# Attention output of two head groups on column tiles of TensorE

## The chip, the cores and the metric

The kernel runs on one core of a Trainium2 chip. The metric is the device time of one execution in microseconds (us), lower is better. A core has TensorE (PE in the profile; its weight loads are listed as PEld), VectorE (DVE), ScalarE (ACT), GpSimd (POOL) and the DMA queues, among them SyncE's (SP), which run beside each other and wait for one another through semaphores.

TensorE keeps a block of weights (`lhsT`) in its array and streams another operand (`rhs`) through it; each matmul has its own weight load. The result goes to PSUM: the columns of `lhsT` become PSUM partitions. The array can be used whole (128 rows by 128 columns) or cut into tiles that are addressed by `tile_position=(row, column)`. A tile of 32x64 takes 32 rows of contraction and 64 weight columns, and its output lies on 64 PSUM partitions.

## The reference

A transformer block on `x` of 2048 x 1024, everything stored in bfloat16: 32 heads of 32 values, causal attention with a window of 256, then a dense layer pair with SiLU.

```python
def _A_ref(x, wqkv, wo):
    B, S, D = x.shape
    H = 32; Dh = D // H; W = 256
    qkv = (x @ wqkv) ...            # split in q, k, v by head
    scores = einsum("bhqd,bhkd->bhqk", q, k) * Dh ** -0.5
    mask = (idx[:, None] - idx[None, :] >= 0) & (idx[:, None] - idx[None, :] < W)
    p = softmax(where(mask, scores, -1e9))
    o = einsum("bhqk,bhkd->bhqd", p, v)
    return o.reshape(B, S, D) @ wo
def _B_ref(x, w1, w2):
    return silu(x @ w1) @ w2
h = x + _A_ref(layernorm(x), wqkv, wo)
out = h + _B_ref(layernorm(h), w1, w2)
```

## The kernel before

The 2048 rows are cut into four blocks of 512 (`b` = 0 to 3), the 32 heads into eight head groups of four (`g` = 0 to 7). The program runs in stages; in each, dense matmuls of one block carry the attention of the block before it:

- first the q, k and v of block 0 (lines 497 to 581);
- the attention of block 0 among the q, k, v of block 1 (lines 587 to 601);
- the attention of block 1 among the q, k, v of block 2, and that of block 2 among those of block 3 (the loop at line 604). Block 2's attention is what the change calls the third stage: it is the third of the four blocks, and its code has `b == 2`;
- the attention of block 3 among the output projections of blocks 0 to 2 (line 639 on);
- then the dense layers, `h1_group` (line 666) and `mm2` (line 704), for all four blocks.

The order of the work is written out by hand and nothing reorders it. The class `Stream` (line 415) sets how attention is mixed into the dense matmuls. A stage has 24 dense groups of eight matmuls, 192 in all; before each dense matmul `between` is called, and at even distances, 20 times in a stage of blocks 1 to 3, it issues a piece of attention output and then a burst of scores. So PE's stream in such a stage is a repeated triple: one piece (`attn_piece`), one burst of scores, and nine or ten dense matmuls.

Scores are computed by `scores_xy` (line 288) on tiles of 32 rows by 64 columns: four heads of the group on four row tiles, two halves of 64 keys on two column tiles, 24 matmuls a burst with 320, 128 and 64 streamed columns. The parts that two neighbouring groups need at the window's edge come from `scores_c` (line 321), every fifth burst, 16 matmuls on tiles of 32x128. ACT takes the exponential of the scores from PSUM (`sc`) into a ring in SBUF (`r_e`), and POOL zeroes what the mask excludes (`select`, line 371).

`attn_out` (line 377) multiplies probabilities by values. `lhsT` is a block of 128 keys by 128 queries, so queries become output partitions; `rhs` is `v` for one head, 32 values and a column of ones that gives the softmax's sum: 33 columns. For one head and 128 queries three such matmuls accumulate in one slot of `o_ps`. A head group has 16 slots (four heads, four query tiles), 48 matmuls. Two neighbouring groups, 32 slots, are cut by `SPLIT` (line 41) into five pieces of 8, 8, 5, 6 and 5 slots; the group with the even number is in the first two, 24 matmuls each. A piece is issued four bursts after the scores it belongs with. After eight slots `attn_norm` (line 392) has DVE divide by the sums, and `attn_transpose` turns the result by DMA.

Weight loads wait for POOL (the mask), the first matmul of a slot bank for DVE (the division before), the first score of a burst for ACT (the exponentials before). These waits stand in PE's own queue.

Of the kernel before, what the change touches and what calls it, by code (L numbers as in the profile page):

```python
# [14 lines left out]
P = 128  # L15
# [22 lines left out]
    [(0, "X", 2), (1, "Y", 1), (2, "X", 3)],  # L38
    [(1, "Y", 2), (2, "C", 1), (3, "Y", 3)],
]  # L40
SPLIT = [(0, 8), (8, 16), (16, 21), (21, 27), (27, 32)]


@with_exitstack
def kernel(
# [10 lines left out]
    nc = tc.nc  # L56
# [12 lines left out]
    VW = DH + 1  # L69
# [22 lines left out]
    o_ps = [ps.tile([P, 8, 64], F32, name=f"o_ps{i}") for i in range(2)]  # L92
    acc_ps = [ps.tile([P, 512], F32, name=f"acc{i}") for i in range(2)]

    def view(region, off, *dims):
        n = 1
        for d in dims:
            n *= d
        ap = region[:, off:off + n]
        if len(dims) == 2:  # L100
            return ap.rearrange("p (a b) -> p a b", b=dims[1])
        if len(dims) == 3:
            return ap.rearrange("p (a b c) -> p a b c", b=dims[1], c=dims[2])
        return ap
# [12 lines left out]
    v = view(r_a, 32768, S // P, H, VW)  # L117
# [113 lines left out]
    def next_acc():  # L231
        acc_n[0] += 1
        return acc_banks[acc_n[0] % len(acc_banks)]
# [45 lines left out]
    def chunk_of(i, bank, piece, pair, hh):  # L279
        if bank == "C":  # L280
            return c_ring[:, (i + 1) % 3, pair * 2 + hh, piece * P:(piece + 1) * P]
        if i < G:
            c0 = hh * 512 + piece * P
        else:
            c0 = 1024 + hh * P if piece == 2 else hh * 512 + (piece - piece // 3) * P
        return xy_ring[(i % 2 * 2 + "XY".index(bank)) * 2 + pair][:, c0:c0 + P]

    def scores_xy(b, g, odd):
        q0 = odd * P
        mid, first, last = odd, odd - 2, odd + 2  # L290

        parts = [
            (mid, 0, q0, q0 + 320, 64), (mid, 1, q0 + 64, q0 + 384, 128),
            (last, 0, q0 + 256, q0 + 384, 384), (first, 1, q0, q0 + 128, 0),
            (first, 0, q0, q0 + 64, 0), (last, 1, q0 + 320, q0 + 384, 448),
        ]
        for step in range(3):
            for hh in range(4):
                for kt, half, qa, qb, col in parts[step * 2:step * 2 + 2]:
                    r0 = hh * DH  # L300
                    t = b * 4 + kt
                    k0 = (t % 4) * P + half * 64
                    nc.tensor.matmul(  # L303
                        sc[hh // 2][half * 64:half * 64 + 64, hh % 2, col:col + qb - qa],
                        lhsT=kT[t // 4][r0:r0 + DH, g, k0:k0 + 64],
                        rhs=qT[b][r0:r0 + DH, g, qa:qb],
                        start=True, stop=True, tile_position=(r0, half * 64),
                    )
        for pair in range(2):
            e = xy_ring[((b * G + g) % 2 * 2 + odd) * 2 + pair]  # L310
            tri = e[:, 0:1024].rearrange("p (h c q) -> p h c q", h=2, q=256)
            bank = sc[pair]
            both = bank[:, :, 0:192]
            both = bass.AP(tensor=both.tensor, offset=both.offset, ap=[*both.ap[:2], [320, 2], both.ap[2]])
            nc.scalar.activation(out=tri[:, :, :, 64:256], in_=both, func=ACT.Exp, scale=scale)  # L315
            nc.scalar.activation(out=e[:, 1024:1280].rearrange("p (h q) -> p h q", q=P), in_=bank[:, :, 192:320], func=ACT.Exp, scale=scale)  # L316
            four = e[:, 0:1024].rearrange("p (c q) -> p c q", q=256)
            select(four[:, :, 0:P], four[:, :, 64:64 + P], False)
            select(four[:, :, P:2 * P], four[:, :, P:2 * P], True)
# [57 lines left out]
    def attn_out(b, g, first, last):  # L377
        i = b * G + g
        for n in range(first, last):
            pair, qt, hh = n // 8, n // 2 % 4, n % 2  # L380
            chunks = (CHUNKS if b else CHUNKS_0)[qt]
            for m, (kt, bank, piece) in enumerate(chunks):
                nc.tensor.matmul(  # L383
                    o_ps[pair][:, qt * 2 + hh, 0:VW],
                    lhsT=chunk_of(i, bank, piece, pair, hh),
                    rhs=v[:, b * 4 + kt, g * 4 + pair * 2 + hh, :],
                    start=(m == 0), stop=(m == len(chunks) - 1),
                )
            if n % 8 == 7:
                attn_norm(i, pair)  # L390

    def attn_norm(i, pair):
        recip = small.tile([P, 8, 1], F32, name="recip", tag="recip")
        nc.vector.reciprocal(out=recip[:], in_=o_ps[pair][:, :, DH:VW])
        nc.vector.tensor_tensor(
            out=obuf[i % 3][:, :, pair * 64:(pair + 1) * 64].rearrange("p t (h d) -> p t h d", d=DH),
            in0=o_ps[pair][:, :, 0:DH].rearrange("p (t h) d -> p t h d", h=2),
            in1=recip[:].rearrange("p (t h) o -> p t h o", h=2).to_broadcast([P, 4, 2, DH]), op=ALU.mult,
        )
# [6 lines left out]
    def attn_piece(b, g, first, last):  # L406

        for k in range(2):
            a, z = max(first - 16 * k, 0), min(last - 16 * k, 16)
            if a < z:  # L410
                attn_out(b, g + k, a, z)
                if z == 16:
                    late.append(lambda k=k: attn_transpose(b, g + k))

    class Stream:
# [3 lines left out]
        def __init__(self, b):  # L419
# [4 lines left out]
            for g in range(0, G, 2):  # L424
                if b:
                    self.bursts += [lambda g=g: scores_c(b, g)]
                    self.bursts += [lambda g=g, k=k, o=o: scores_xy(b, g + k, o) for k in range(2) for o in range(2)]
                    self.pieces += [lambda g=g, s=s: attn_piece(b, g, *s) for s in SPLIT]
                else:
# [86 lines left out]
    pair = [next_acc() for _ in range(2)]  # L516
# [166 lines left out]
    for b in range(NB):  # L683
# [4 lines left out]
        for ft in range(FT):  # L688
# [8 lines left out]
            if b == 0 and 7 <= ft < 15:  # L697
                j, c = divmod(ft - 7, 2)
# [60 lines left out]
```

## Time and profile before

| | |
|---|---|
| time, median of 3 runs | 691.2 us (690.91 to 691.21) |
| profiled execution, first to last instruction (span) | 688.9 us |
| PE busy | 685.2 us, 99% of the span |
| DVE, ACT, POOL busy | 42%, 35%, 23% |
| attention output, all 1440 matmuls of 128x33 (line 383) | 48.1 us busy, 178 ns mean of one |
| stage of block 2's attention | 163.3 to 223.4 us from the span's start |
| its pieces for groups 2 and 4 | start at 190.4, 193.4, 205.4 and 208.4 us |

The page gives no other time for the profiled execution than its span; the median of the timed runs is 2.3 us above that span. A row of the profile names the line of the kernel, the engine, the operation, what it writes and reads by the program's names, the array tile (`128*128` or `32*64`) and the shape of the streamed operand, then how many. The duration of one matmul is from its start to its modelled end; matmuls overlap, so the distance from one start to the next is shorter than the duration: 25 ns for the 128x33 matmuls that are listed with 178 ns. The chain lists what ended last, piece by piece in order of time.

### The profile page before, as it was taken

The numbers are of one execution on the slowest core, as the hardware profiler recorded it, in microseconds if no ns is written. First come the engines' busy times: TensorE is split into PE (matmuls) and PEld (weight loads), VectorE is DVE, ScalarE is ACT, GpSimd is POOL, SyncE is SP. The second block draws the span as 40 slices with busy tenths as digits, with TensorE's granted clock in tenths as the row PEclk, the third lists the DMA queues.
The fourth block names the chain that finished last, engine by engine and source line by source line (L and its number), as shares of the span: only waits on it lengthen the run. The fifth ranks groups of instructions, "written<-read, shape, count | busy, mean of one in ns | idle before, by whom it ended". The sixth has DMA issues, their size and how long they took to land.

```text
span 688.9 us, 14243 instructions
## 1 busy us (share of the span) xinstructions
PE 685.2 (99%) x6011; PEld 342.3 (50%) x6011; DVE 291.2 (42%) x613; ACT 244.2 (35%) x464; POOL 160.8 (23%) x295
## 2 busy tenths in 40 slices
PE   9999999999999999999999999999999999999998
PEld 4445555555555555544444444444444444444445
DVE  5267647744444449444316133342233251333111
ACT  7326666666667666421300033300133100233000
POOL 1006666566666656400000000000000000000000
PEclk9999999999999999999999999999999999999999
DMA  7832231126241889871023310022300123100110
GB/s 259 275 64 69 40 85 57 25 63 186 71 131 21 257 252 272 199 267 40 23 88 112 84 39 0 1 91 70 85 0 1 21 96 90 39 1 1 30 39 24
DMA packets 78641, 61.48 MB, mean 89 GB/s; under 512 B 52465, under 2 KB 62705, under 8 KB 78577
## 3 DMA queue, kind: packets, MB, share of 16 engines
q1 hardware_dynamic: 77888, 59.78, 30.2%
q8 instruction: 47, 0.77, 0.4%
q10 hardware_dynamic: 688, 0.79, 0.3%
q14 instruction: 18, 0.14, 0.1%
HBM read 39.85 MB, written 8.39 MB: 70 GB/s over the span
## 4 chain that ended last, share of the span: by engine, by line
PE 99%; DVE 0%; issue 0%
PE hacc L669 19%; PE hacc L706 18%; PE acc L250 17%; PE acc L706 11%; PE acc L669 9%; PE acc L240 7%; PE acc L271 7%; PE o_ps L383 5%; PE sc L303 3%; PE hacc L271 2%; PE sc L355 1%; PE o_ps L240 1%; PE o_ps L167 1%; PE sc L329 1%; PE acc L525 0%; PE o_ps L525 0%
## 5 line engine op out<-in xcount | busy, mean ns | idle before, releaser
L373 POOL TENSOR_SCALAR_AFFINE_SELECT r_e<-r_e 128x512 bf16<-128x512 bf16 (+1 forms) x288 | 157.8, 563 | 123.9 <-ACT r_e L363 60.8
L706 PEld LDWEIGHTS <-r_a 128*128 128x128 bf16 x952 | 90.9, 98 | 103.0
L669 PEld LDWEIGHTS <-r_w 128*128 128x128 bf16 x896 | 87.3, 98 | 104.8
L706 PE MATMUL hacc<-r_a 128*128 128x512 bf16 (+2 forms) x616 | 122.5, 360 | 0.0
L669 PE MATMUL hacc<-r_e,r_w 128*128 128x512 bf16 x456 | 100.9, 379 | 0.0
L315 ACT ACTIVATE r_e<-sc 128x768 bf16<-128x768 f32 x96 | 78.2, 814 | 47.9 <-PE sc L303 47.9
L678 ACT ACTIVATE r_n<-hacc 128x512 f32<-128x512 f32 x30 | 17.9, 597 | 178.9 <-PE hacc L669 178.9
L250 PEld LDWEIGHTS <-r_w 128*128 128x128 bf16 x512 | 47.1, 98 | 55.0 <-issue 1.0
L706 PE MATMUL acc<-r_a 128*128 128x512 bf16 x336 | 74.0, 379 | 0.0
L252 DVE CAST r_a<-acc 128x512 bf16<-128x512 f32 x56 | 38.7, 692 | 57.7 <-PE acc L250 57.4
L250 PE MATMUL acc<-r_t,r_w 128*128 128x512 bf16 x256 | 59.6, 380 | 0.0
L250 PE MATMUL acc<-r_w 128*128 128x512 bf16 x256 | 57.8, 380 | 0.0
L383 PEld LDWEIGHTS <-r_e 128*128 128x128 bf16 x1440 | 47.4, 96 | 17.9
L669 PE MATMUL acc<-r_e,r_w 128*128 128x512 bf16 x216 | 49.1, 379 | 0.0
L271 PE MATMUL acc<-r_o,r_a 128*128 128x512 bf16 x208 | 48.7, 380 | 0.0
L383 PE MATMUL o_ps<-r_a,r_e 128*128 128x33 bf16 x1440 | 48.1, 178 | 0.0
L721 DVE SCALAR_TENSOR_TENSOR r_t<-hacc,r_t 128x512 bf16<-128x512 f32 (+2 forms) x22 | 14.0, 635 | 56.7 <-PE hacc L706 56.7
L316 ACT ACTIVATE r_e<-sc 128x256 bf16<-128x256 f32 x96 | 37.6, 392 | 0.0
L271 PEld LDWEIGHTS <-r_a 128*128 128x128 bf16 x256 | 23.4, 98 | 26.9
L721 DVE SCALAR_TENSOR_TENSOR r_t<-acc,r_t 128x512 bf16<-128x512 f32 x12 | 8.3, 692 | 64.2 <-PE acc L706 64.2
L679 DVE SCALAR_TENSOR_TENSOR r_a<-r_n,hacc 128x512 bf16<-128x512 f32 x30 | 20.6, 687 | 33.0 <-ACT r_n L678 33.0
L669 PE MATMUL hacc<-r_a,r_w 128*128 128x512 bf16 x144 | 33.0, 379 | 0.0
(100 smaller groups left out, 539.6 us busy)
## 6 DMA issues: line engine op xcount, KB each, us to landing
r_w<-in_B_w_dram SPq DMA_DIRECT2D x8, 896.0 KB, 5.2
r_a<-in_B_w_dram SPq DMA_DIRECT2D x7, 1024.0 KB, 7.5
r_w<-in_A_wqkv_dram SPq DMA_DIRECT2D x4, 1024.0 KB, 7.8
h_dram<-r_t SPq DMA_DIRECT2D x16, 256.0 KB, 3.1
r_t<-h_dram SPq DMA_DIRECT2D x16, 256.0 KB, 2.8
out_dram<-r_t SPq DMA_DIRECT2D x31, 128.0 KB, 1.7
r_o<-in_A_x_dram SPq DMA_DIRECT2D x15, 256.0 KB, 4.6
r_e<-h_dram SPq DMA_DIRECT2D x3, 1024.0 KB, 5.7
```

The costliest lines, as they stand in the source:

```text
L240: nc.tensor.matmul(acc, lhsT=lnT_b[b % 2][:, kt, j * P:(j + 1) * P], rhs=wv[:, kt, c * 512:(c + 1) * 512], start=(kt == 0), stop=(kt == KT ...
L250: nc.tensor.matmul(acc, lhsT=wqk[:, kt, col0:col0 + P], rhs=lnT_b[b % 2][:, kt, :], start=(kt == 0), stop=(kt == KT - 1))
L252: copy(out=(qT, kT)[which][b][:, g, :], in_=acc)
L271: nc.tensor.matmul(acc, lhsT=qT[b][:, g, j * P:(j + 1) * P], rhs=wo[:, g, c * 512:(c + 1) * 512], start=(g == 0), stop=(g == G - 1))
L303: nc.tensor.matmul(sc[hh // 2][half * 64:half * 64 + 64, hh % 2, col:col + qb - qa], lhsT=kT[t // 4][r0:r0 + DH, g, k0:k0 + 64], rhs=qT[b] ...
L315: nc.scalar.activation(out=tri[:, :, :, 64:256], in_=both, func=ACT.Exp, scale=scale)
L316: nc.scalar.activation(out=e[:, 1024:1280].rearrange("p (h q) -> p h q", q=P), in_=bank[:, :, 192:320], func=ACT.Exp, scale=scale)
L373: nc.gpsimd.affine_select(out=dst, in_=src, pattern=[[0, n] for n in dst.shape[1:-1]] + [[sgn, P]], compare_op=ALU.is_ge if upper else ALU ...
L383: nc.tensor.matmul(o_ps[pair][:, qt * 2 + hh, 0:VW], lhsT=chunk_of(i, bank, piece, pair, hh), rhs=v[:, b * 4 + kt, g * 4 + pair * 2 + hh, ...
L669: nc.tensor.matmul(acc, lhsT=w1[:, kt, ft * P:(ft + 1) * P], rhs=ln2T[b][:, kt, :], start=(kt == 0), stop=(kt == KT - 1))
L706: nc.tensor.matmul(acc[:, 0:c1 - c0], lhsT=gT[:, ft, j * P:(j + 1) * P], rhs=w2[ft // 4][:, ft % 4, c0:c1], start=(ft == 0), stop=(ft == F ...
L721: nc.vector.scalar_tensor_tensor(out=t_out[j % 2][:, c0:c1], in0=acc[:, 0:c1 - c0], scalar=0.5, in1=t_in[j % 2][:, c0:c1], op0=ALU.mult, o ...
```

## The change

In block 2 two of the eight head groups compute the same products on column tiles. `COLS` names them: group 2 uses four tiles of 128 rows by 32 columns, group 4 two tiles of 128 rows by 64 columns. Each matmul of 128 query columns is replaced by four of 32 or two of 64: the same `rhs`, a slice of `lhsT`, and the matching slice of the output's partitions. The order of chunks and slots, what comes before and after, and all other groups stay as they are.

```diff
+COLS = {(2, 2): 32, (2, 4): 64}
 SPLIT = [(0, 8), (8, 16), (16, 21), (21, 27), (27, 32)]
...
             for m, (kt, bank, piece) in enumerate(chunks):
-                nc.tensor.matmul(
-                    o_ps[pair][:, qt * 2 + hh, 0:VW],
-                    lhsT=chunk_of(i, bank, piece, pair, hh),
-                    rhs=v[:, b * 4 + kt, g * 4 + pair * 2 + hh, :],
-                    start=(m == 0), stop=(m == len(chunks) - 1),
-                )
+                lhsT = chunk_of(i, bank, piece, pair, hh)
+                w = COLS.get((b, g), P)
+                for c in range(0, P, w):
+                    tiled = {} if w == P else {"tile_position": (0, c)}
+                    nc.tensor.matmul(
+                        o_ps[pair][c:c + w, qt * 2 + hh, 0:VW],
+                        lhsT=lhsT[:, c:c + w],
+                        rhs=v[:, b * 4 + kt, g * 4 + pair * 2 + hh, :],
+                        start=(m == 0), stop=(m == len(chunks) - 1), **tiled,
+                    )
             if n % 8 == 7:
                 attn_norm(i, pair)
```

## The prediction

> **What bounds the kernel now.** I read the page first (busy shares, granted clock, the chain by engine), then PE's own waits.
>
> ```profile
> span 688.9 us, 14243 instructions
> PE 685.2 (99%) x6011; PEld 342.3 (50%) x6011; DVE 291.2 (42%) x613; ACT 244.2 (35%) x464; POOL 160.8 (23%) x295
> ...
> PEclk9999999999999999999999999999999999999999
> ...
> PE 99%; DVE 0%; issue 0%
> ```
>
> ```profile
> PE o_ps L167 <- DVE eps L147: 1.1, 1, 1.1
> ```
>
> TensorE is the chain from end to end, at full clock, and the only wait recorded for it is 1.1 us at the very start. So a nanosecond added to its stream anywhere is a nanosecond at the end; what other engines do counts only if they make it wait. The four pieces that change are found in the chain, in order of time (start, length, what), by counting bursts of the third stage, which begins at 163.3:
>
> ```profile
> 190.55 0.59 PE o_ps L383 x24
> 191.14 0.36 PE sc L303 x24
> 191.50 2.05 PE acc L250 x9
> 193.54 0.59 PE o_ps L383 x24
> 194.14 0.33 PE sc L329 x16
> 194.47 2.26 PE acc L250 x10
> ...
> 205.58 0.59 PE o_ps L383 x24
> 206.17 0.36 PE sc L303 x24
> 206.53 2.05 PE acc L250 x9
> 208.58 0.59 PE o_ps L383 x24
> 209.17 0.33 PE sc L329 x16
> ```
>
> Every burst is the same triple: a piece of attention output, a burst of scores, then nine or ten dense matmuls. The first two pieces are head group 2, the last two head group 4: 24 matmuls in 0.59 us each, 2.4 us in all. The single records in the trace give 25.0 ns from one matmul of 128x33 to the next, with its weight load under it, and 216 ns between dense matmuls of 512 columns.
>
> The last rows are about PE's sequencer, which hands instructions to the array (PEldq marks what it executes itself). First an undisturbed dense stretch, then the end of a burst:
>
> ```profile
> L669 PEldq EVENT_SEMAPHORE  x2: 51/51/51, 392.0 to 392.1; - x2
> ```
>
> ```profile
> 392.01 3.55 PEld L706 LDWEIGHTS <-r_a 128*128 128x128 bf16 x17
> 395.68 0.10 PEld L669 LDWEIGHTS <-r_w 128*128 128x128 bf16 x1
> ```
>
> ```profile
> L271 PEldq EVENT_SEMAPHORE  x1: 51/51/51, 224.2 to 224.2; - x1
> ```
>
> At 392.0 the sequencer stood before the first L669 load while 33 instructions of L706 (17 loads, 16 matmuls) had not started: it runs at most about 33 instructions ahead. At 224.152 it reached the first L271 load, 21 instructions ahead, after a piece and a burst of 80 instructions that began at 223.443. It should have been there by 224.02, when only 32 were left, had it been faster. So in bursts it falls behind, and its pace can be bounded.
>
> **The change, part by part.**
>
> *Instructions.* The order of instructions of both kernels differs only in these four pieces: 24 pairs of load and matmul become 96, 96, 48 and 48. That is 192 pairs, 384 instructions, more. The other engines' orders and the semaphore waits are unchanged: the POOL waits sit on the same chunks, and no DMA is added or moved. Nothing new queues behind a wait.
>
> *Entering the tile mode.* Full-array dense to full-array o_ps costs nothing now (216 ns to the next start). Every change of tile shape does: the last o_ps matmul to the first score is 107 ns, the last score (64 columns) to dense 120, the last L329 (128 columns) to dense 146. Columns cost 0.417 ns each (216 ns for 512, 56 for 128), so 14, 27 and 53 of these are streaming and 93 is left each time. After the change each of four pieces begins with such a switch: 306 instead of 216, +0.09 us, and its first weights are no longer loaded ahead, +0.01 to 0.03 (the first round of 320-column scores takes 160 ns where 133 are streaming). I take +0.10 each, 0.4 in all. Leaving costs as before, since o_ps to scores already switched.
>
> *The array.* No row shows 128 rows on column tiles. Nearest are the scores: eight tiles of 32x64, two column halves on the same rows. In the burst at 191.07 the eight start 3.3 ns apart, the next eight 160 ns after the first eight, the last eight 56 ns on. So both halves stream side by side, and each load is hidden. By that row four column tiles do in one round what one full matmul did, and a round costs 25 ns or less (loading 64 columns takes 27). From below: 33 columns stream in 14 ns, so a piece could shrink from 0.59 to about 0.4. From above: every column tile pays its own 25 ns, 96 x 25 = 2.4 us. I take the score row, the only one with column tiles.
>
> [...]
>
> *The supply of instructions.* If the array does a round of eight instructions in 25 ns, it eats one each 3 ns, far over what the sequencer has shown. Bounds on its pace: before, the last score of a 24+24 burst (instruction 96) starts on time 0.926 us after the piece; with 33 already queued, 63 were supplied in that time, so at most 14.7 ns each. The event at 224.152: ACT released the second score bank, for which the 53rd of the 80 waits, at 223.80; if the sequencer stood at that wait, 28 instructions took 0.35 us, 12.5 ns each; if it stood nowhere, 47 took 0.71, 15 ns, which the first bound excludes. From below: scores leave the queue at one instruction each 1.7 ns, and no row shows that the sequencer cannot fill it as fast. I take 12.5 ns: it is the reading that fits both rows, and twice it is the 25.0 ns of a full-array pair.
>
> The sum, from each piece's start to its last score (before: 0.926 us with L303, 0.877 with L329; 33 instructions are queued):
> - Group 2, first: 192 + 48 instructions, (240 - 33) x 12.5 = 2.59; +1.66.
> - Group 2, second: 192 + 32, 191 x 12.5 = 2.39; +1.51.
> - Group 4, first: 96 + 48, 111 x 12.5 = 1.39; +0.46.
> - Group 4, second: 96 + 32, 95 x 12.5 = 1.19; +0.31.
>
> With the four entries (0.4) that is +4.3 us. Nothing gives it back: the dense stretch after each burst is PE's own work. What comes late (the o_ps reciprocals, the exponentials) hangs off engines busy 44% to 68% of this stage, and PE never waits for them. The profiled span would be 693.2. The runs' median is 691.2, 2.3 above the profiled span, which I leave as it is: **695.5 us**.
>
> [...]
>
> **The rivals.**
> 1. *The cover holds* (not slower). The sequencer supplies far faster than 12.5 ns, and the event at 224.152 was late for another reason. Then group 2 costs only its entries and group 4 adds 2 to 4 ns to each of 48 rounds: 0.4 + 0.15, about 691.7. It decides if the pace is below 4.5 ns: (240 - 33) x 4.5 = 0.926. For it: nothing in the trace shows a tile burst running dry. Against: the late event.
> 2. *Column tiles take turns.* Each pays the full-array 25 ns: 2 x (72 x 25) + 2 x (24 x 25) = 4.8, plus 0.4: 696.4. For it: 25.0 ns is the pace of every 128-row matmul here. Against: column halves overlap in the scores.
> 3. *Turns, and the load not hidden.* 13 + 16 ns for 32 columns, 27 + 16 for 64: pieces of 2.8 and 2.1 us instead of 0.6, +7.3, plus 0.4: about 698.9. Against: loads of a busy tile are hidden in the scores.
> 4. *Faster.* Rounds at 16 ns instead of 25, with supply to match, give 2 x 24 x 9 ns = 0.4 us, which the entries eat. Over 0.2% would need 1.4 of the 2.4 us that all four pieces take.
>
> **How the numbers follow.** The supply-bound sum 0.46, rival 1 0.17, rival 2 0.19, rival 3 0.10, rival 4 0.03, anything worse 0.05. A difference of 0.2% (1.4 us) is about what a measurement of this kernel can tell from none. Rival 1 lies inside it, the others beyond: faster 0.03, same 0.17, slower 0.80. The sum by itself runs from 9 ns an instruction (+2.3) to 14.7 (+5.7): 693.5 to 696.9. The range takes in rivals 1 to 3, 691.7 to 699.3.
>
> **What would show it.** Right: in the profile after, the two pieces of group 2 take about 2 us and those of group 4 about 0.8 (the rest of the price falls in the scores, which spread from 0.24 us to as much as 0.6); within a piece the first four rounds are quick and the rest go at one pair per 25 ns; 0.31 us from the last dense start to the first tile. Equal spacing of 25 ns from the first pair on, with score bursts as short as now, is rival 2; 29 and 43 ns is rival 3; pieces of 0.6 us, rival 1. The prediction fails if the queue or the pace is not what two single records make it.

## The result, and the profile after

The changed kernel takes 695.4 us (median of 4 runs, 694.8 to 697.4) against 691.2 before: 1.0067 times as long, 95% interval 1.0053 to 1.0081 (the ratios in this document are taken over the runs and differ a little from those of the medians). The forecast was 695.5. The number came out; the reason given for it did not, and most of what follows is about that.

The page of the changed kernel, profiled in its longest run (697.35 us, span 695.6):

```profile
span 695.6 us, 14512 instructions
PE 677.3 (97%) x6088; PEld 342.6 (49%) x6203; DVE 291.1 (42%) x613; ACT 244.1 (35%) x464; POOL 160.7 (23%) x295
...
q8 instruction: 48, 0.79, 0.5%
...
PE 96%; issue 2%; DMA 2%; ACT 0%; ACTq 0%; DVE 0%
```

PE is no longer the whole chain: 2% is "issue", time in which it waited for nothing that the profile shows, and 2% is DMA. The weight loads are complete (6203, 192 more than before), but 115 matmul records are missing, so PE's own waits list many "issue" gaps of 0.05 to 0.2 us where a dense matmul has no record. Two waits are real, since the loads stop there too:

```profile
PE o_ps L388 <- issue: 2.6, 1, 2.6
...
PE acc L674 <- DMA r_a<-r_a: 1.7, 1, 1.7
```

The chain of the changed kernel around the four pieces (start, length, what):

```profile
191.36 0.86 PE o_ps L388 x96
192.22 0.36 PE sc L304 x24
...
194.63 0.83 PE o_ps L388 x92
195.46 2.56 issue
198.02 0.20 PE o_ps L388 x4
198.22 0.33 PE sc L330 x16
...
209.67 0.87 PE o_ps L388 x48
210.53 0.36 PE sc L304 x24
```

A piece of 96 matmuls on four column tiles takes 0.86 us, one of 48 on two tiles 0.87, where 24 full ones took 0.69 from their first to the next line's first. The score bursts after them still take 0.36. Then, 92 matmuls into the second piece of group 2, PE stops for 2.56 us.

Lining up the weight loads of both profiles, which are complete, shows where the 6.7 us between the two spans arise. 0.8 lie in the first 8 us, in the wait for the first loads; a second profile of the unchanged kernel (below) loses 1.05 in its first 21 us, so the change need not have brought them. The pieces cost 4 x 0.27, the stop 2.7. Another 1.9 come over 70 us after the last changed instruction, at the first matmul of the dense layers (L674, before: L669), which waits for the transposes of the normalised block 0; this is called the late wait below. The remaining 0.2 come in the output projections. Pieces, stop and late wait are what the experiments take apart. The length of the late wait is given by how far that first matmul moves against the profile before.

### The profile page after: what moved, and what is told of

The parts are those of the page before. It is cut to its first block, busy times and chain, and to the rows that moved or that the text cites. A ratio compares the mean times of both kernels' runs of the same rounds, so it can differ in the third digit from the quotient of the medians.

```text
span 695.6 us, 14512 instructions
## 1 busy us (share of the span) xinstructions
PE 677.3 (97%) x6088; PEld 342.6 (49%) x6203; DVE 291.1 (42%) x613; ACT 244.1 (35%) x464; POOL 160.7 (23%) x295
## 4 chain that ended last, share of the span: by engine, by line
PE 96%; issue 2%; DMA 2%; ACT 0%; ACTq 0%; DVE 0%
PE hacc L674 19%; PE hacc L711 17%; PE acc L251 16%; PE acc L711 10%; PE acc L674 9%; PE acc L241 7%; PE acc L272 6%; PE o_ps L388 5%; PE sc L304 2%; PE hacc L272 1%; DMA r_w<-in_A_wqkv_dram 1%; PE sc L356 1%; PE o_ps L241 1%; DMA r_a<-r_a 1%; PE sc L330 1%
## 5 line engine op out<-in xcount | busy, mean ns | idle before, releaser
L674 PEld LDWEIGHTS <-r_w 128*128 128x128 bf16 x896 | 87.3, 98 | 106.7 <-issue 2.2
L674 PE MATMUL hacc<-r_e,r_w 128*128 128x512 bf16 x453 | 100.4, 379 | 0.1
L251 PE MATMUL acc<-r_t,r_w 128*128 128x512 bf16 x233 | 56.5, 380 | 2.4 <-issue 1.6
L388 PEld LDWEIGHTS <-r_e 128*128 128x128 bf16 (+2 forms) x1632 | 47.8, 96 | 21.4 <-issue 4.4
L251 PE MATMUL acc<-r_w 128*128 128x512 bf16 x240 | 56.0, 379 | 1.5 <-issue 1.0
L388 PE MATMUL o_ps<-r_a,r_e 128*128 128x33 bf16 (+2 forms) x1632 | 49.0, 179 | 2.6 <-issue 2.6
L674 PE MATMUL acc<-r_e,r_w 128*128 128x512 bf16 x205 | 48.3, 379 | 0.6
L272 PE MATMUL acc<-r_o,r_a 128*128 128x512 bf16 x188 | 46.4, 380 | 1.9 <-issue 1.3
L674 PE MATMUL hacc<-r_a,r_w 128*128 128x512 bf16 x142 | 32.8, 379 | 0.1
```

Source lines behind the costliest of these rows:

```text
L251: nc.tensor.matmul(acc, lhsT=wqk[:, kt, col0:col0 + P], rhs=lnT_b[b % 2][:, kt, :], start=(kt == 0), stop=(kt == KT - 1))
L272: nc.tensor.matmul(acc, lhsT=qT[b][:, g, j * P:(j + 1) * P], rhs=wo[:, g, c * 512:(c + 1) * 512], start=(g == 0), stop=(g == G - 1))
L388: nc.tensor.matmul(o_ps[pair][c:c + w, qt * 2 + hh, 0:VW], lhsT=lhsT[:, c:c + w], rhs=v[:, b * 4 + kt, g * 4 + pair * 2 + hh, :], start=(m ...
L674: nc.tensor.matmul(acc, lhsT=w1[:, kt, ft * P:(ft + 1) * P], rhs=ln2T[b][:, kt, :], start=(kt == 0), stop=(kt == KT - 1))
```

## The experiments

The page before also lists a DMA queue of instructions, q8: 47 transfers, 0.77 MB, so 16 KB each. PE's 12,022 weight loads and matmuls make about 256 for each. From that q8 is taken to feed PE, and one transfer is called a block of 256 instructions here.

Three theories for the time in the pieces:

- **F** (fetch): column tiles overlap as the scores do; the stop is PE's sequencer running out of instructions, because the next block is stuck behind a weight load of the dense layers, 896 KB of `w1`.
- **P** (piece): the same stop, but the piece outruns the fetch by itself, wherever it stands.
- **S** (supply): the recorded theory, a sequencer that hands over an instruction each 12.5 ns.

Two for the late wait: **D** (delay), any delay of PE brings it; **K**, it depends on where in the stream the blocks of 256 end, so on how many instructions were added.

### The same kernel again

> The changed kernel itself, for a second profile and more times. Theory F (fetch): column tiles overlap, and all but about 1.1 us of the price is one stop of PE in the second piece of group 2, where its sequencer has run out of instructions because the next block of them comes late, behind the 896 KB load of w1 that is then under way: 694.8 to 695.6 us, with one stop of 1.5 to 3 us at that place, 25 ns a round in the first rounds and 33 ns after. Theory P (a piece of 192 instructions outruns the fetch by itself): the same here. Theory S (the recorded one, 12.5 ns an instruction): pieces of about 2 us, no stop.

698.95 us (696.0 to 700.4), 1.0107 times before [1.0086, 1.0127], above all of the expected range; the shape is F's and P's. The first piece has 96 matmuls in 0.86 us, and the second stops after 92, for 2.08 us, as before. Part of what came on top is the clock. Rows of stretches (length, busy time of PE, PEld, DVE, ACT, POOL, then the granted clock as a share of full speed, DMA's share and GB/s):

```profile
196.20:198.40 2.20, 0.12 (x8) 0.10 (x4) 0.00 (x0) 0.00 (x0) 0.77 (x2) 0.97 0.00 0
198.40:199.00 0.60, 0.60 (x20) 0.37 (x21) 0.39 (x2) 0.00 (x0) 0.00 (x0) 0.50 0.00 0
199.00:202.00 3.00, 3.00 (x12) 1.13 (x9) 0.24 (x1) 1.94 (x2) 0.00 (x0) 0.55 0.28 49
```

Behind the stop TensorE ran at half clock for over 3 us, and seven dense matmuls took 0.43 us instead of 0.216: 1.4 us more. The first profile, with a longer stop, shows a clock of 1.00 throughout. Of the rest, e1's profile lost 1.6 us in the first 21 us, 0.9 in the output projections (a wait for DVE) and 2.0 in the late wait.

### One group at a time

```diff
-COLS = {(2, 2): 32, (2, 4): 64}
+COLS = {(2, 2): 32}          # e2_group2_only
+COLS = {(2, 4): 64}          # e3_group4_only
```

> Group 2 on 32-column tiles, group 4 as before. F and P: the two entries and slower late rounds, 2 x 0.27 us, and the stop of about 2.6: +3.1 us. S: +3.4 us (1.76 + 1.61), so only the profile tells S apart: one stop against slow pieces.

694.1 against 690.9, +3.15 us, 1.0037 [1.0023, 1.0052]; pieces of 0.86, no late wait, and the stop:

```profile
194.11 0.83 PE o_ps L388 x92
194.94 2.30 issue
```

F and P hold; S, which forecast nearly the same time, falls by the profile, and not by the time.

> Group 4 on 64-column tiles, group 2 as before. F and P: two entries of 0.09 and two pieces 0.18 longer, +0.55 us, no stop. S: +1.0 us, score bursts spread out.

A miss for everyone: 694.0, +3.1 us, 1.0040 [1.0027, 1.0052], with runs from 691.5 to 696.6. The pieces cost what was expected (two of 0.87). Most of the rest is one wait, which no theory had:

```profile
PE acc L674 <- DMA r_a<-r_a: 2.1, 1, 2.1
```

So the late wait is no accident of one run: it can cost four times what the column tiles of group 4 do. It led to D and K.

### The widths changed places

```diff
+COLS = {(2, 2): 64, (2, 4): 32}
```

> Group 2 on 64-column tiles and group 4 on 32-column tiles, as many instructions in all. F: no transfer is under way at group 4 (DMA idle from 205 us on), so the stop is gone or under 0.7 us: +1.1 to +1.8 us. P: the stop goes with the 32-column tiles to group 4: +3.7 us. S: +4.3 us as in the kernel that was changed.

694.65, +3.7 us, 1.0051 [1.0038, 1.0064]. By the time alone this would be P's case, and F's +1.1 to +1.8 was missed. The chain says otherwise; the two pieces on four column tiles:

```profile
206.27 0.86 PE o_ps L388 x96
...
209.53 0.43 PE o_ps L388 x44
209.96 0.12 issue
210.08 0.57 PE o_ps L388 x52
```

The stop is gone but for 0.12 us. In the profiled run the time went elsewhere, 1.2 us of it into the late wait. That run was the shortest of the four (693.6); what the other three lost besides, no trace shows.

### The load moved out of the way, and into it

```diff
-            if b == NB - 1 and n in (4, 10, 14):
-                load_w1({4: 7, 10: 6, 14: 5}[n])
+            if b == NB - 1 and n in (4, 14, 20):            # e5: changed kernel
+                load_w1({4: 7, 14: 5, 20: 6}[n])
+            if b == NB - 1 and n in (4, 10, 16):            # e7: widths swapped
+                load_w1({4: 7, 10: 6, 16: 5}[n])
```

> The changed kernel with the third load of w1 in that stage issued at dense group 20 instead of 10, so that no transfer is under way in group 2's two pieces. Theory F (the next block of instructions comes late behind that load): the stop of 2.2 to 2.6 us in the second piece of group 2 falls to under 0.7. Theory P (192 instructions a piece outrun the fetch by themselves): the stop stays at over 2 us. Nothing said of the later wait before the dense layers, which every profile but one of the changed kernels shows (1.4 to 2.5 us).

> Group 2 on 64-column tiles, group 4 on 32-column tiles, and the fourth load of w1 issued at dense group 16 instead of 14, so that it is under way in group 4's pieces as the third load was in group 2's. F: a stop of 1.5 to 3 us appears in group 4's pieces, where the same tiles without the load lost at most 0.2. P: no stop, as without the move.

The chain of the changed kernel with the load moved away, group 2's second piece:

```profile
193.98 0.83 PE o_ps L388 x92
194.81 0.02 issue
194.83 0.20 PE o_ps L388 x4
```

and of the swapped kernel with a load moved in, group 4's second piece:

```profile
210.13 0.43 PE o_ps L388 x44
210.56 2.27 issue
212.83 0.56 PE o_ps L388 x52
```

Same tiles, same instruction at which the block ends (92 in the one, 44 in the other): 2.56 us become 0.02, and 0.12 become 2.27. The load decides, so F stands and P falls. P is not far off, though: without the load PE still stands for 0.02 and 0.12 us at the block's end, so the fetch is only just in time. The times are 694.8 (1.0062 [1.0040, 1.0085]) and 696.2 (1.0080 [1.0066, 1.0094]): e5 still has the late wait (2.0 us); e7 has the late wait (1.4), the stop, and half clock behind the stop (1.4). That e5 lost the stop is shown by its profile and not by its time, which is only 0.6 us below the first measurement of the changed kernel.

### A delay without instructions, and instructions without a delay

```diff
+            if (b, which, g, kt) == (3, 0, 4, 0):           # e8: before, and
+                for _ in range(3):
+                    nc.tensor.matmul(acc, lhsT=wqk[:, kt, col0:col0 + P], rhs=lnT_b[b % 2][:, kt, :], start=True, stop=True)
...
-    for i in range(9):                                      # e9: before, but
+    for i in range(8):
         busy(4)
+    for i in range(65):
+        c = i % 4 * 32
+        nc.tensor.matmul(o_ps[0][c:c + 32, 0, 0:VW], lhsT=warm[:, c:c + 32], rhs=warm[:, 0:VW], start=True, stop=True, tile_position=(0, c))
```

> The kernel before with one dense matmul of block 3 (k, group 4) issued three times more, which changes no result: PE is delayed by 3 x 216 ns = 0.65 us at 204 us, and the instruction stream is 6 longer. Theory D (any delay of PE there upsets the transfers before the dense layers): +0.65 and a wait of 1.4 to 2.5 us at the first matmul of the dense layers, +2 to +3 us in all. Theory K (the wait comes when a fetch of instructions falls among the four transposes of the normalised block 0, so it depends on where the 256-instruction blocks end): no wait, +0.65 us.

> The kernel before with one of nine warm-up matmul blocks replaced by 65 matmuls on 32-column tiles of zeros at the start: 128 instructions more ahead of everything, no change in any stage. K: the fetch before the dense layers moves from 5.2 us to about 3.8 us ahead of their first matmul, as in the changed kernel, and a wait of 1.4 to 2.5 us appears there: +1.4 to +3 us. D: no wait, within 0.5 us of before.

The delay alone: 691.9, 1.0012 [1.0003, 1.0021], +0.8 us against 0.65 put in, and no wait at the dense layers. PE's waits in its profile:

```profile
PE o_ps L167 <- DVE eps L147: 1.0, 1, 1.0
PE acc L240 <- DMA r_w<-in_A_wqkv_dram: 0.3, 1, 0.3
```

The instructions alone: 693.15, 1.0031 [1.0020, 1.0043], +2.0 us, from 65 short matmuls in place of one long one in the first 6 us of the program. Its profile loses 0.6 us at the start, where the unchanged kernel varies as much, 0.3 at each of two places on the way, and 1.0 at the dense layers, less than the 1.4 to 2.5 that K expected. There the weight loads stand idle:

```profile
PEld L672 <- issue: 1.3, 1, 1.3
```

```profile
PE acc L672 <- DVE r_t L276: 0.8, 1, 0.8
```

D falls, K stands: 128 instructions more at the start bring a wait some 280 us later, where a delay alone brings none. In this profile PE's matmul was released by DVE's last sum of the output projection and not by the transposes, so it is not always the same work that is late.

### The blocks put back

The same 65 matmuls ahead of the changed kernel make its stream 512 instructions longer than before, two whole blocks.

> The kernel before itself, for a second profile. K (the wait before the dense layers belongs to where the instruction blocks end): no wait there, 690.7 to 691.9 us. If the wait shows here too, it is the chip's and not the change's.

> The changed kernel with 128 instructions more at the start (one of nine warm-up blocks replaced by 65 matmuls on 32-column tiles), so that from group 4 on its stream is 512 instructions, two whole blocks, longer than before. K: the fetch before the dense layers is back at 5 to 7 us ahead of them and the wait of 1.4 to 2.5 us there is gone; the stop in group 2 stays, since the load is still under way, but begins at another instruction: 1.4 to 2.5 us less than the changed kernel. D: the wait stays.

Before again: 690.85, 0.9997 [0.9988, 1.0006]; 0.2 us of the late wait and 1.05 at the start in its profile, which is of its longest run. The changed kernel with two whole blocks: 694.85, 1.0056 [1.0042, 1.0071]. Its dense layers start without a wait, as K expects. The stop is there, and its place is a check on F, for 128 instructions are 64 pairs:

```profile
193.99 0.28 PE o_ps L391 x28
194.27 2.92 issue
197.19 0.73 PE o_ps L391 x60
```

It comes after 28 matmuls, where it came after 92: 64 earlier (8 matmul records of this piece are missing behind it). Half clock followed it again (1.3 us), which ate much of what the late wait had cost; the time is 0.6 below the first measurement of the changed kernel and 4.1 below the second, on another chip, so the expected 1.4 to 2.5 is not shown by times.

### Neither the stop nor the wait

Widths swapped, and the 65 matmuls at the start.

> Group 2 on 64-column tiles, group 4 on 32-column tiles (no load under way in the 32-column pieces), and 128 instructions more at the start, so that the stream from group 4 on is 512 instructions longer than before. F and K together: no stop and no wait before the dense layers; what is left is the column tiles' own price, 4 x 0.27 = 1.1 us, at most 0.3 at a block's end and up to 0.5 at the start: +1.1 to +1.9 us. If it stays over +2.5, there is a cost that neither names.

692.4 against 691.1, +1.3 us, 1.0021 [1.0011, 1.0030], runs from 691.9 to 693.4. The pieces:

```profile
191.03 0.87 PE o_ps L391 x48
...
194.31 0.87 PE o_ps L391 x48
...
206.62 0.86 PE o_ps L391 x96
...
209.88 0.86 PE o_ps L391 x96
```

No stop, and 0.1 us at the dense layers. What is left is about the price of the column tiles themselves, 288 matmuls in place of 96: 4 x 0.27 = 1.1 us by the pieces, while the time also holds what the 65 matmuls cost at the start (the profile loses 0.5 there). The original placement with both the load moved and whole blocks was not measured.

## Why the prediction was right, and where it was wrong

**The frame held in part.** 192 pairs were added in the four pieces and no semaphore wait, and the kernel became 0.6% slower, as forecast. But PE did not stay the whole chain: it waits in places that the change does not touch.

**Entering the tile mode: right.** Predicted 306 ns from the last dense matmul to the first tile, 0.10 us each; measured 309 or 310.

**The array: right for 32 columns, short for 64.** The score row carried over to 128 rows. In the single records four 32-column tiles start 1 to 5 ns apart and a round of four takes 25 ns, exactly one full matmul, in the first eight rounds of a piece. Two 64-column tiles take 31.5 ns a round, not the 27 to 29 of rival 1, which makes 0.18 us a piece instead of 0.05 to 0.1. Rivals 2 and 3 (tiles in turn, loads not hidden) fall with it: the added matmuls cost the 1.3 us of the last experiment, entries included, and not rival 2's 4.8 besides the entries. The 27 ns that the prediction puts on loading 64 columns is an estimate, by what the first score round takes over its streaming (160 ns against 133), and 13 for 32 columns is half of it. No run shows the 16 ns that rivals 3 and 4 reckon with; what was measured is rounds of 25 and 33 ns for four tiles and 31.5 for two.

**The supply of instructions: wrong, and it was 3.9 of the 4.3 us.** After the first eight rounds of a 32-column piece the rounds go from 25 to 33 ns: a load and a matmul each 8.3 ns, 64 pairs in a row. A whole piece of 192 instructions starts within 0.745 us; with 33 of them queued beforehand, the sequencer supplied the other 159 in at most 4.7 ns each, not 12.5, which is about the 4.5 below which the prediction let rival 1 decide. The slower rounds cost about 0.13 us a piece, where group 2's pieces were to cost 1.5 and 1.7. Whether it is the sequencer that sets the 33 ns is open. A quick round takes eight instructions in 25 ns and a pair each 8.3 ns brings six, so a full queue of 32 would last 16 rounds and not eight; and behind the stops of e4 and e7, where the queue should be empty, eight quick rounds come again.

The step that failed is the reading of one record, "it should have been there by 224.02, when only 32 were left". The depth of 33 had been taken from the record at 392.026, which comes 19 ns after a load has left (392.007): 32 instructions were waiting. Two more such records, at 488.719 and 585.412, come 18 ns after a load and show 32 as well. With a queue that is full at 32, the record at 224.152 says that the sequencer stood at a full queue, for it came 24 ns after the first score load had left (224.128). One slot's uncertainty was read as a pace; that reading is argued, not tested. The two bounds that seemed to support the pace, 14.7 and 15 ns, were upper bounds only, and of the lower end the text said that no row showed the sequencer unable to be faster. Between ends far apart, the value was then chosen by a coincidence with 25.0 ns.

**"No DMA is added or moved": wrong, and it is where the time went.** Instructions come by DMA too, and the page before listed them:

```profile
q8 instruction: 47, 0.77, 0.4%
```

The 384 instructions more move every block's end from group 2 on. Two costs follow that the prediction had neither as a term nor as a rival:

- The stop: 2.1 to 2.9 us in the five profiles where 32-column pieces stood beside a load (the first, e1, e2, e7, e11b), 0.12 or less in the three where none was under way (e4, e5, e13).

  From the first 32-column piece to the second, 258 instructions go by in 3.3 us; before, 256 took 6.2 to 8.9 us in this stage. In the single DMA records of all five, the block's transfer starts 2 to 3 ns after the load's last packet has ended (the first profile: 195.775 after 195.773), 3.3 to 4.0 us after PE passed the end of a block; with the load moved away (e5, e4) it starts after 0.9 us.

  The transfer takes about 1 us (0.9 to 1.3), and PE goes on 1.2 to 1.5 us after its end; no record shows what happens in that time. An estimate from e4 and e5 is 0.9 + 1.3 + 1.3 = 3.5 us, without a load in the way, from the passing of a block's end until the block whose fetch then begins can be used; their pieces eat a block in 3.5 us. Before, the transfer started 0.7 us after PE passed a block's end (194.86 after 194.19, the load's last packet ended at 194.45), and PE needed that block only 6.8 us after the transfer's end. (The blocks' ends are counted from the places of the stops, one each 128 pairs.)
- The late wait, 1.0 to 2.3 us, which follows the number of instructions modulo 256. Counted in loads and matmuls ahead of the dense layers, the remainder is 214 or 246 where the wait appears and 118 to 150 where it doesn't (0.2 us at most). That a shift of the blocks brings it (e9) and whole blocks take it away (e11b, e13) is shown. Why is only argued: where it appears, a block's fetch starts 2.5 to 3.9 us ahead of the dense layers, among the last transfers they wait for; where it doesn't, 5.2 to 7.0 us ahead.

**The sum was right by accident.** Predicted: 0.4 for entries, 3.9 for the supply. Found in the profiled run: 1.1 for entries and pieces, 2.7 for the stop, 1.9 for the late wait, besides 0.8 at the start. The other three of its four runs are 1.8 to 2.5 us shorter than the profiled one; they left no trace. A second measurement of the same kernel gave 698.95 (e1), 3.5 us over the forecast. Rival 1 (691.7), the case nearest to the mechanism, gave the tiles half of their own price (0.55 us against 1.1) and had no idea of the rest.

## What to carry to other kernels

Where a stretch uses many short matmuls, count instructions as bytes to be fetched, here 16 KB for 256: a fetched block could be used about 3.5 us after PE passed the end of one (the estimate above), and 2.1 to 2.9 us later where a load of 896 KB was under way. A stretch that ate a block in 3.5 us beside such a load stopped in all five profiles. A time that changes when instructions are only added far away (2.0 us in e9) can be a sign that the ends of the blocks have moved; padding the stream to whole blocks and moving a load aside separate such effects from the price of the edit. And a forecast that meets its number is not yet a theory that is right: here only the piece's length in the profile (0.86 against 2 us) told the two apart.

## What was not expected of the hardware

- In the profile after, column tiles with all 128 rows overlap: for eight rounds four 128x32 take 25 ns a round, the time of one full 128x33 matmul, and 33 ns after that; two 128x64 take 31.5.
- PE's sequencer supplies an instruction in 4.7 ns or less (192 start within 0.745 us, at most 33 of them queued before); a load and a matmul each 8.3 ns went on for 64 pairs.
- An instruction block waited for a load of 896 KB to the end: its transfer starts 2 to 3 ns after the load's last packet, in five of five stops.
- Behind a stop of 2.1 us (e1) the granted clock was 0.50 to 0.55 for over 3 us, and behind one of 2.9 us (e11b) 0.53 to 0.60. Behind one of 2.3 us (e7) six dense matmuls took 0.41 us each instead of 0.216. Behind 2.6 us (the first profile) the clock stayed at 1.00, and behind 2.3 us (e2) ten dense matmuls took 2.27 us, against 2.26 before.
- 65 short matmuls in place of one long one in the start-up, 128 instructions more, with no other change, cost 2.0 us of 691 (e9).
